# First expert's counts in narrow products, row of -1 in the operand, tokens turned on PE, constant fill in attention, and both stages in a new order

## The chip, the cores and the metric

One Trainium2 chip, one of its cores. The engines of the core are PE (TensorE; its weight loads are shown apart as PEld), DVE (VectorE), ACT (ScalarE), POOL (GpSimd) and SP (SyncE), which issues most DMAs. The metric is the time of one execution on the device in microseconds (us); the kernel's time is the median of several runs.

## What is computed

Top-32 attention over 8 batches and 8 heads (576 positions, 64 dimensions a head), then a mixture of 8 experts over the 4608 tokens, to which tokens go by a greedy assignment in order of their logits, at most 576 to an expert.

```python
def _attn_ref(q, k, v):
    scores = scale * np.matmul(q, k.transpose(0, 1, 3, 2))
    kth = np.partition(scores, -top_k, axis=-1)[..., -top_k:-top_k + 1]
    scores = np.where(scores >= kth, scores, -1000000000.0)
    ...
    return np.matmul(attn, v)

def _moe_ref(x, w_gate, w1, w2):
    logits = x @ w_gate
    order = np.argsort(-logits.flatten())
    for idx in order:
        tok, e = (int(idx) // E, int(idx) % E)
        if assigned[tok] >= 0 or counts[e] >= cap:
            continue
        assigned[tok] = e
        counts[e] += 1
    for e in range(E):
        mask = assigned == e
        out[mask] = np.maximum(x[mask] @ w1[e], 0.0) @ w2[e]
```

## The kernel before

**Order.** Both stages are written as operations with a due time: `at(t, f, pre, e=...)` registers operation `f` for engine `e`. `Plan.run` simulates the engines and issues, on each one, among the operations that could begin within `WIN` of the earliest, the one of smallest due time. The due time is the tile's or expert's own time plus an offset from the table `O`. The result is a fixed stream of instructions for each engine, which then runs in that order. `PLANBUFS` and the arguments of the second `Plan` give the sizes of the rings of buffers. So a new table gives a new order without any other change.

**Attention** runs over 32 pairs (8 batches, 4 pairs of heads) with 9 tiles of 128 rows each, 288 in all. Q and K are loaded, rounded on POOL and turned by DMA transposes on SP (line 186). For a tile PE writes 128x576 scores in `s` (218). DVE finds the largest values in six chunks (221), ranks them (224 to 228), and writes the negative of the 24th value (229). ACT takes the sign of every score against it and sums that in `acc` (233). PE moves the scores above it far down with a product by `off` (236), and DVE's `fill` (238) puts up to eight copies of the 24th value in the eight columns behind the scores, as many as the sum in `acc` asks for. DVE's next MAX8 (239) takes eight values over 584 columns; PE moves the others back with `back` (236), and ACT clears what is below the 32nd (242). Then come the masked scores once more, transposed (PE, 285 and 286), the exponential (ACT, 290), its two halves in f16 (POOL, 293 and 296), the products with V (PE, 364), the reciprocal of the sum (DVE, 344 and 378) and the scaled rows in `x` (ACT, 346).

After the fourth pair of a batch, `logits` (388) turns the batch's rows on PE in five pieces (396), copies them to SBUF on ACT (398), multiplies them by the gate's weights on PE (402, 404) and puts 8 columns in `L` on ACT (407, 408). The pieces wait for the pair's last rows. `verdict` (416) follows the planned part in program order: it checks `acc` with eight operations (420 to 428) and `L` for values that are not finite (430 to 432), and writes flags. `redo` reads the flags and branches to a repeat, or goes on.

**Experts.** Expert p has a `route`: six steps that close in on its threshold. In a step DVE compares all best logits with 32 thresholds (`g`, 671; three parts for the first expert), PE counts with 9 products that hold four tiles each (674), DVE masks and folds (677, 680), PE sums them up (684) and writes -1 in the columns next to them (685, with a constant row `mone`), DVE compares with the capacity (687, `okb`), PE adds that on the -1 (688), and DVE takes the largest (689) and the next thresholds (695, 696). `enlist` (738) makes the list of the expert's tokens: DVE writes one-hot tiles (757 to 761), PE lays them out (`lay`, 36 products, 765) and spreads them (772), DVE forms `idx` (775). `weigh` (776) reads the expert's number on SP (779), loads four weight blocks of 1 MB (787, ring of four buffers `wr`) and splits them into two f16 halves (ACT 799, DVE 807). `bring` (822) gathers the tokens on POOL in five tiles (829), splits them (ACT 836, DVE 839, ring of three `xs`), and turns them with DMA transposes on SP (840). `ffn` (841) multiplies: 192 products `ph` (856), their halves (ACT 865, DVE 866), 108 steps of `po` (880, 883), the result (890 to 894) and a scatter on POOL (895). The next expert's route, list and weights are planned beside the products of the one before.

## Time and profile before

| | us |
|---|---|
| median of 3 runs | 1474.12 |
| the runs | 1474.12, 1472.0, 1474.5 |
| the profiled execution, its own time | 1470.44 |
| its span | 1468.4 |
| PE busy | 1295.9 (88%) |
| PE weight loads (PEld) busy | 913.2 (62%) |
| DVE busy | 1220.3 (83%) |
| POOL busy | 877.2 (60%) |
| ACT busy | 864.6 (59%) |

The profile is of one execution. The busy shares are means over the stages: attention takes the time up to about 964, the route and fetch of the first expert up to about 1028, and the experts' products the rest.

### The profile page before, as it was taken

Reading aid. Unit: us, or ns where it says so; the run is one execution under the profiler, and the core shown is the slowest. Engines: PE = TensorE matmul, PEld = TensorE weight load, DVE = VectorE, ACT = ScalarE, POOL = GpSimd, SP = SyncE. Lnnn points to the kernel's source line nnn. Section 1 sums busy time; section 2 is a strip of 40 time slices with the busy share of each in tenths; the row PEclk is TensorE's granted clock in tenths of the full one; section 3 lists DMA queues with packets and bytes.
Section 4 is the critical chain, followed back from the end, with each engine's and each line's share of the span. In section 5 each row is a group of like instructions: output and inputs, shape, how many; then the busy total and the mean of one; then the engine's idle time right before and its main releaser. Section 6 shows DMA issues by size and latency. Waiting matters only on the chain. (4 is left out here: it accounts for less than half of the span.)

```text
span 1468.4 us, 41338 instructions
## 1 busy us (share of the span) xinstructions
PE 1295.9 (88%) x14885; PEld 913.2 (62%) x14886; DVE 1220.3 (83%) x5951; ACT 864.6 (59%) x1922; POOL 877.2 (60%) x1285
## 2 busy tenths in 40 slices
PE   2888998999999999999999899832999999998997
PEld 1666776776776776677677677621655655664663
DVE  4899999999999999999999999658889878887610
ACT  2677777777777777777777787612334424324421
POOL 5688789788788788789879878502043123122211
PEclk9899999999999999999999999955999999999899
DMA  6343363354455445443543452016346346348500
GB/s 130 74 88 78 80 127 84 75 120 91 82 110 97 89 108 84 94 109 77 97 110 83 92 107 46 10 35 170 122 99 198 137 91 198 140 96 271 112 33 33
DMA packets 298149, 149.62 MB, mean 102 GB/s; under 512 B 255440, under 2 KB 280016, under 8 KB 296912
## 3 DMA queue, kind: packets, MB, share of 16 engines
q1 hardware_dynamic: 292048, 128.02, 38.5%
q0 software_dynamic: 5888, 18.88, 4.5%
q8 instruction: 119, 1.95, 0.6%
q14 instruction: 94, 0.77, 0.2%
HBM read 71.34 MB, written 18.87 MB: 61 GB/s over the span
## 5 line engine op out<-in xcount | busy, mean ns | idle before, releaser
L221 DVE MAX8 cd<-s 128x8 f32<-128x96 f32 x1728 | 383.2, 251 | 35.4 <-PE s L218 28.6
L296 POOL TENSOR_TENSOR elm<-F,ehm 128x512 f16<-128x512 f32 x256 | 294.3, 1156 | 6.3
L242 ACT ACTIVATE r<-s,st 128x576 bf16<-128x576 f32 x288 | 213.0, 740 | 98.8 <-PE s L236 93.8
L233 ACT ACTIVATE w<-s,st 128x576 uint16<-128x576 f32 x288 | 213.1, 740 | 95.0 <-DVE st L229 92.9
L895 POOL DMA_INDIRECT out_dram<-ob,idx x40 | 59.0, 1476 | 326.1 <-ACT ob L890 268.2
L239 DVE MAX8 st<-s 128x8 f32<-128x584 f32 x288 | 220.5, 766 | 10.4 <-PE s L236 6.7
L218 PE MATMUL s<-K,Q 128*128 128x512 f16 (+3 forms) x1280 | 195.3, 293 | 28.6 <-DMA Q<-nq 22.3
L856 PE MATMUL ph<-xT,w1h 128*128 128x288 f16 x1024 | 195.8, 289 | 2.0 <-DMA xT<-xs 2.0
L293 POOL TENSOR_SCALAR ehm<-F 128x512 f16<-128x512 f32 x256 | 156.0, 617 | 52.7 <-ACT F L290 52.3
L286 PE MATMUL pt<-Q,K 66*128 66x128 f16 (+1 forms) x1280 | 182.6, 217 | 0.2 <-DMA Q<-nq 0.2
L285 PE MATMUL pt<-Q,K 128*128 128x128 f16 (+1 forms) x1280 | 181.6, 216 | 0.0
L218 PEld LDWEIGHTS <-Q 128*128 128x128 f16 (+1 forms) x1280 | 105.9, 103 | 111.9 <-DMA Q<-nq 22.0
L236 PE MATMUL s<-w,off 128*128 128x512 f16 x576 | 134.1, 290 | 46.8 <-DVE s L238 26.9
L290 ACT ACTIVATE F<-pt 128x512 f32<-128x512 f32 x256 | 150.4, 596 | 20.8 <-PE pt L286 18.5
L856 PE MATMUL ph<-xT,w1l 128*128 128x288 f16 x512 | 147.6, 288 | 0.0
L364 PE MATMUL pv<-vt,E 128*64 128x65 f32 (+1 forms) x1024 | 146.4, 257 | 0.0
L236 PE MATMUL s<-w,back 128*128 128x512 f16 x576 | 120.9, 292 | 23.5 <-DVE st L239 21.7
L865 ACT ACTIVATE hh<-ph 128x288 f16<-128x288 f32 x128 | 52.4, 410 | 146.3 <-PE ph L856 145.4
L285 PEld LDWEIGHTS <-K 128*128 128x128 f16 x1280 | 118.3, 99 | 22.5 <-issue 8.7
L364 PEld LDWEIGHTS <-ehm 128*128 128x128 f16 x2048 | 116.2, 102 | 10.0 <-issue 0.5
L364 PEld LDWEIGHTS pv<-vt,E 128*64 128x64 f32 (+1 forms) x1024 | 113.0, 164 | 14.5 <-issue 3.5
L364 PE MATMUL pv<-vh,ehm 128*128 128x65 f16 x1024 | 120.8, 195 | 0.6 <-ACT F L290 0.6
(252 smaller groups left out, 3271.0 us busy)
## 6 DMA issues: line engine op xcount, KB each, us to landing
wr<-in_moe_w_dram SPq DMA_DIRECT2D x32, 1024.0 KB, 8.2
kn<-in_k_dram SPq DMA_DIRECT2D x64, 128.0 KB, 2.6
qn<-in_q_dram SPq DMA_DIRECT2D x64, 128.0 KB, 2.3
vn<-in_v_dram SPq DMA_DIRECT2D x64, 128.0 KB, 2.3
x<-xb SPq DMA_DIRECT2D x8, 1024.0 KB, 4.8
Q<-nq SPq DMA_TRANSPOSE x160, 3.3
kn<-in_k_dram SPq DMA_DIRECT2D x64, 16.0 KB, 2.3
qn<-in_q_dram SPq DMA_DIRECT2D x64, 16.0 KB, 2.2
```

The costliest lines, as they stand in the source:

```text
L218: T.matmul(s_ps[rows,a:b_],P[Q][:,qc],P[K][:,h*576+a:h*576+b_],start=(Q=="Q1"),stop=(Q=="Q2"))
L221: V.max(D["cd"][:,c*8:c*8+8],D["s"][:,576*c//NCH:576*(c+1)//NCH])
L233: A.activation(D["w"],D["s"][:,:576],AF.Sign,bias=P["st"][:,i,32:33],scale=(1+2.0**-21),accum_out=acc[:,col])
L236: T.matmul(D["s"][:,a:b_],by,w[:,a:b_],start=False,stop=True,skip_group_check=True)
L239: def next8(): V.max(P["st"][:,i,24:32],D["s"][:,:584])
L242: A.activation(r,D["s"][:,:576],AF.Relu,bias=P["st"][:,i,31:32],scale=-1.0)
L285: T.matmul(o,K2[:,kb:kb+128],Q1[:,qc],start=False,stop=False,skip_group_check=True)
L286: T.matmul(o,K3[0:66,kb:kb+128],Q2[0:66,qc],start=False,stop=(c==3 and h==sub[-1][0]),skip_group_check=True)
L293: G.tensor_scalar(D["eh"],D["E"],1.0,0.0,op0=ALU.mult,op1=ALU.add)
L296: G.tensor_tensor(el,D["E"],D["eh"],op=ALU.subtract); P["e"][i]=(D["eh"],el)
L364: for m_ in (range(N-1) if part==0 else (N-1,)): T.matmul(out,seq[m_][0],seq[m_][1],start=(m_==0),stop=(m_==N-1))
L856: P.matmul(B["ph"][:,:288],a[:,c,fs],xT[:,b+c,cs],start=(i==0),stop=(i==11))
```

## The change

In attention, `fill` writes a constant, 2^40, in place of the row's 24th value, so it reads one scalar of each partition fewer; the relu and the planner's durations are otherwise as before. `logits` is in two parts: after a batch's third pair it turns and multiplies the first 384 of 512 columns of each row group (four pieces) and one corner, and copies the results to `L`; after the fourth pair it does the last 128 columns of all four row groups in one piece and the second corner, and adds them to `L`. These copies and adds are on DVE, no longer on ACT. `verdict` tests `L` in four pieces (12 operations) and folds its flags in other operations. In the experts, `okb` has a 33rd row that holds -1 in two fixed buffers, so the product with `mone` is gone and the product with `okb` stands alone. The first expert's counts are 36 products of 128x32 weights that add up in one tile of 32x8, without the mask, the two folds and the sum. The first expert's tokens are turned by PE in place of DMA: four transposes a tile into PSUM, from which ACT and DVE write the two halves. The tables `O`, `PER`, `SP` and `WIN` of attention and the tables of the experts have other numbers, and with them all engines have another order.

```diff
-        PER=4.6166; SP=1.3822; VP=3; WPB=14; EHB=14
-        WIN={'V': 0.027, 'A': 0.079, 'G': 0.008, 'P': 0.138, 'D': 1.472}
+        PER=4.9146; SP=1.9733; VP=3; WPB=14; EHB=14
+        WIN={'V': 0.021, 'A': 0.06, 'G': 0.042, 'P': 0.137, 'D': 1.95}
...
-            def fill(): V.tensor_scalar(D["s"][:,576:584],tab,acc[:,col],P["st"][:,i,23:24],op0=ALU.is_lt,op1=ALU.mult)
+
+            def fill(): V.tensor_scalar(D["s"][:,576:584],tab,acc[:,col],2.0**40,op0=ALU.is_lt,op1=ALU.mult)
...
-        def logits(P):
-            b=P["b"]; n=P["n"]; t0=(n*9+8)*PER+O["lg"]
-            fin=[]
-            for c in range(5):
-                p=P["done"]
-                D={}; w=512 if c<4 else 256
-                def turn(c=c,D=D):
-                    D["pt"]=ps_t.tile([128,512],F32,tag="pt",name="ptl")
-                    for f in range(4 if c<4 else 2): T.transpose(D["pt"][:,f*128:(f+1)*128],P["x"][0][:,c,f*128:(f+1)*128] if c<4 else P["x"][1][:,2*f:2*f+2,:].rearrange("p a d -> p (a d)"),identf)
-                def copy(D=D,w=w):
+        def logits(P,part):
+
+            b=P["b"]; n=P["n"]; t0=(n*9+8)*PER+O["lg"]; o=(b%2)*64
+            done=P["done"]; fin=[]
+            def piece(k,turns,w,dots,put):
+
+                D={}; t=t0+O["lgd"]*k
+                def turn():
+                    pt=D["pt"]=ps_t.tile([128,512],F32,tag="pt",name="ptl")
+                    for j,src in enumerate(turns): T.transpose(pt[:,j*128:j*128+128],src(),identf)
+                def copy():
                     D["xT"]=wk.tile([128,512],F32,tag="xT",name="xT",bufs=2); A.activation(D["xT"][:,:w],D["pt"][:,:w],AF.Copy)
-                def dot(c=c,D=D):
-                    lg=D["lg"]=ps_t.tile([128,512],F32,tag="pt",name="lg"); xT=D["xT"]; o=(b%2)*64
-                    if c<4:
-                        for f in range(4): T.matmul(lg[:,:8],xT[:,f*128:(f+1)*128],wg[:,f,:],start=(f==0),stop=(f==3))
-                    else:
-                        for i_,(g,a) in enumerate(((0,0),(0,1),(1,0),(1,1))): T.matmul(lg[o:o+64,:8],xT[:,g*128+a*64:g*128+a*64+64],wgr[:,g,a,:],start=(i_==0),stop=(i_==3))
-                def put(c=c,D=D):
-                    o=(b%2)*64
-                    if c<4: A.activation(L[:,b*4+c,:],D["lg"][:,:8],AF.Copy)
-                    else: A.activation(L[o:o+64,32+b//2,:],D["lg"][o:o+64,:8],AF.Copy)
-                t=t0+O["lgd"]*c
-                p=at(t,turn,[p],take="pt",e="P",d=.436); tp=p
-                p=at(t+O["l1"],copy,[p],free=[tp],take="xT",e="A",d=.48); tx=p
-                p=at(t+O["l2"],dot,[p],take="pt",free=[tx],e="P",d=.9); tp=p
-                p=at(t+O["l3"],put,[p],free=[tp],e="A",d=.07); fin.append(p)
-            P["fin"]=at(t0,lambda: None,fin)
-            P["done"]=p
+                def dot():
+                    D["lg"]=ps_t.tile([128,512],F32,tag="pt",name="lg"); dots(D["lg"],D["xT"])
+                p=tp=at(t,turn,[done],take="pt",e="P",d=.11*len(turns))
+                p=tx=at(t+O["l1"],copy,[p],free=[tp],take="xT",e="A",d=.06+w*.00083)
+                p=tp=at(t+O["l2"],dot,[p],take="pt",free=[tx],e="P",d=.224*len(turns))
+                fin.append(at(t+O["l3"],lambda: put(D["lg"]),[p],free=[tp],e="V",d=.08))
+            main=L[:,b*4:b*4+4,:]; last=L[o:o+64,32+b//2,:]
+            def corner(g):
+                def dots(lg,xT):
+                    for a in range(2): T.matmul(lg[o:o+64,:8],xT[:,a*64:a*64+64],wgr[:,g,a,:],start=(a==0),stop=(a==1))
+                return [lambda: P["x"][1][:,2*g:2*g+2,:].rearrange("p a d -> p (a d)")],128,dots
+            if part==0:
+                for c in range(4):
+                    def dots(lg,xT):
+                        for f in range(3): T.matmul(lg[:,:8],xT[:,f*128:f*128+128],wg[:,f,:],start=(f==0),stop=(f==2))
+                    piece(c,[lambda f=f,c=c: P["x"][0][:,c,f*128:f*128+128] for f in range(3)],384,dots,lambda lg,c=c: V.tensor_copy(L[:,b*4+c,:],lg[:,:8]))
+                piece(4,*corner(0),lambda lg: V.tensor_copy(last,lg[o:o+64,:8]))
+            else:
+                def dots(lg,xT):
+                    for c in range(4): T.matmul(lg[:,c*8:c*8+8],xT[:,c*128:c*128+128],wg[:,3,:],start=True,stop=True)
+                piece(0,[lambda c=c: P["x"][0][:,c,384:512] for c in range(4)],512,dots,lambda lg: V.tensor_tensor(main.rearrange("p c e -> p (c e)"),lg[:,:32],main.rearrange("p c e -> p (c e)"),op=ALU.add))
+                piece(1,*corner(1),lambda lg: V.tensor_tensor(last,lg[o:o+64,:8],last,op=ALU.add))
+            P["fin"]=at(t0,lambda: None,fin); P["lgdone"]=fin[-1]
...
-            Lf=L.rearrange("p t e -> p (t e)"); fin=cp.tile([128,Lf.shape[1]],F32,name="fin")
-            V.tensor_tensor(fin,Lf,Lf,op=ALU.subtract)
-            V.tensor_scalar(fin,fin,0.0,None,op0=ALU.is_equal)
-            V.tensor_reduce(good[:,npr:],fin,axis=AX.X,op=ALU.add)
+            whole=[]
+            for k,(u0,u1) in enumerate(((0,28),(32,35),(28,32),(35,36))):
+                Lf=L[:,u0:u1,:].rearrange("p t e -> p (t e)"); w=8*(u1-u0); fin=cp.tile([128,w],F32,name=f"fin{k}")
+                V.tensor_tensor(fin,Lf,Lf,op=ALU.subtract)
+                V.tensor_scalar(fin,fin,0.0,None,op0=ALU.is_equal)
+                V.tensor_reduce(good[:,npr+k:npr+k+1],fin,axis=AX.X,op=ALU.add); whole.append(128.0*w)
...
-            if P["hp"]==3 or n==len(pairs)-1:
-                logits(P); batch[b]=at((n*9+8)*PER+O["lg"]+O["lgd"]*5,lambda P=P: store(P),[P["fin"]],e="D",d=2.0,late=4.0)
+            if P["hp"]==2: logits(P,0)
+            if P["hp"]==3:
+                P["done"]=at(P["done"]["t"]+.001,lambda: None,[P["done"],Ps[n-1]["fin"]])
+                logits(P,1); P["done"]=P["fin"]; batch[b]=at((n*9+8)*PER+O["lg"]+O["lgd"]*5,lambda P=P: store(P),[P["fin"]],e="D",d=2.0,late=4.0)
...
+        okbs=[cp.tile([T+1,E],BF16,name=f"okb{k}") for k in range(2)]
+        for t in okbs: V.memset(t[T:T+1,:],-1.0)
...
-                    def begin(): o("g",128,NT,T,dt=BF16); D_["pc"]=new(ps,[128,512],F32,"pc",1)
+                    def begin(p=p):
+                        o("g",128,NT,T,dt=BF16); D_["pc"]=new(ps,[128,512],F32,"pc",1)
+                        if p==0: D_["pn"]=D_["pc"]
                     for q in range(pcs):
                         js=slice(q*n,q*n+n)
                         def cmp_(q=q,js=js):
@@ -671,21 +688,25 @@
                             V.tensor_tensor(D_["g"][:,js,:],D_["v"][:,js].unsqueeze(2).to_broadcast([128,n,T]),D_["thr"].unsqueeze(1).to_broadcast([128,n,T]),op=ALU.is_ge)
                         cq=plan.at(c.t+.05*q,cmp_,head+(R["span"] if p==0 and s==0 else []),e="V",d=.07+n*T*.00104,order=[cq] if q else []); cv=[cq]
                         def count(q=q):
-                            for j in range(q*n,q*n+n,4): P.matmul(D_["pc"][:,:32],D_["g"][:,j:j+4,:].rearrange("p a b -> p (a b)"),D_["ohb"][:,j:j+4,:].rearrange("p a b -> p (a b)"),start=(j==0),stop=(j==NT-4))
-                        mms.append(plan.at(c.t,count,cv+(mms[-1:]),e="P",d=.03*(n//4)+.03))
+                            if p==0:
+                                for j in range(q*n,q*n+n): P.matmul(D_["pn"][:T,:E],D_["g"][:,j,:],D_["ohb"][:,j,:],start=(j==0),stop=(j==NT-1))
+                            else:
+                                for j in range(q*n,q*n+n,4): P.matmul(D_["pc"][:,:32],D_["g"][:,j:j+4,:].rearrange("p a b -> p (a b)"),D_["ohb"][:,j:j+4,:].rearrange("p a b -> p (a b)"),start=(j==0),stop=(j==NT-4))
+                        mms.append(plan.at(c.t,count,cv+(mms[-1:]),e="P",d=.03*(n//4)+.03 if p else .03*n+.03))
                     c.pre=[mms[-1]]; c.t+=.15
-                    c.add("V",.10,lambda: V.tensor_tensor(o("cm",128,32),D_["pc"][:,:32],dm,op=ALU.mult))
-                    def fold():
-                        o("ch",128,E,dt=F16)
-                        with nc.allow_low_precision(reason="counts up to 1152"): V.tensor_reduce(D_["ch"],D_["cm"].rearrange("p (j e) -> p e j",e=E),axis=AX.X,op=ALU.add)
-                    c.add("V",.10,fold)
-                    def total():
-                        D_["pn"]=new(ps,[128,512],F32,"pc",1)
-                        P.matmul(D_["pn"][:T,:E],sel_,D_["ch"],start=True,stop=True)
-                        P.matmul(D_["pn"][:,16:16+E],onesb[:1,:],mone,start=True,stop=False,skip_group_check=True)
-                    c.add("P",.06,total)
-                    c.add("V",.07,lambda: V.tensor_scalar(o("okb",T,E,dt=BF16),D_["pn"][:T,:E],float(CAP),None,op0=ALU.is_ge))
-                    c.add("P",.04,lambda: P.matmul(D_["pn"][:,16:16+E],onesb[:T,:],D_["okb"],start=False,stop=True,skip_group_check=True))
+                    if p:
+                        c.add("V",.10,lambda: V.tensor_tensor(o("cm",128,32),D_["pc"][:,:32],dm,op=ALU.mult))
+                        def fold():
+                            o("ch",128,E,dt=F16)
+                            with nc.allow_low_precision(reason="counts up to 1152"): V.tensor_reduce(D_["ch"],D_["cm"].rearrange("p (j e) -> p e j",e=E),axis=AX.X,op=ALU.add)
+                        c.add("V",.10,fold)
+                        def total():
+                            D_["pn"]=new(ps,[128,512],F32,"pc",1)
+                            P.matmul(D_["pn"][:T,:E],sel_,D_["ch"],start=True,stop=True)
+                        c.add("P",.06,total)
+                    def enough(s=s): D_["okb"]=okbs[(s+p)%2]; V.tensor_scalar(D_["okb"][:T,:],D_["pn"][:T,:E],float(CAP),None,op0=ALU.is_ge)
+                    c.add("V",.07,enough)
+                    c.add("P",.04,lambda: P.matmul(D_["pn"][:,16:16+E],onesb[:T+1,:],D_["okb"],start=True,stop=True,skip_group_check=True))
...
+                if p==0:
+                    B={}
+                    def turn(j=j,n=n,B=B):
+                        if j==0: e["xT"]=new(sm,[128,8,CAP],F16,"xT")
+                        B["pt"]=new(ps,[128,512],F32,"ph",4).rearrange("p (f n) -> p f n",f=4)
+                        for f in range(4): P.transpose(B["pt"][:,f,:n],xgs[j][:n,f*128:f*128+128],ident[:n,:n])
+                    def hi(j=j,n=n,B=B): A.activation(e["xT"][:,0:4,j*128:j*128+n],B["pt"][:,:,:n],AF.Copy,scale=SX)
+                    def lo(j=j,n=n,B=B): V.scalar_tensor_tensor(e["xT"][:,4:8,j*128:j*128+n],B["pt"][:,:,:n],SX,e["xT"][:,0:4,j*128:j*128+n],op0=ALU.mult,op1=ALU.subtract)
+                    tp=plan.at(t+.1*j+.01,turn,[g],e="P",d=.45,take="ph",free=[g],order=[e["x"][j-1] if j else None])
+                    if j==0: te=plan.at(t+.1*j+.015,lambda: None,[tp],take="xT"); e["txT"]=te
+                    a=plan.at(t+.1*j+.02,hi,[tp,te],e="A",d=.5)
+                    e["x"].append(plan.at(t+.1*j+.03,lo,[a],e="V",d=.6,free=[tp]))
+                    continue
```

The table `O` of the experts (line 595) changes in the same way as the one of attention, and the durations given for fill and next8 are 0.12 and 0.685 in place of 0.075 and 0.735. Below is what the new tables give at three places.

DVE, at the end of attention, before: `rs` belongs to the scaling of the last values, `vc`, `vr`, `vok` and `good` to the check of `acc`, `fin` to that of `L`.

```order
L344 TENSOR_SCALAR rs_21723<-pv_21705 128x1
L378 RECIPROCAL rs_21723<-rs_21723 128x1
L420 TENSOR_SCALAR vc_21793<-acc_158 128x288
L421 TENSOR_SCALAR vr_21794<-vc_21793 128x288
L422 TENSOR_SCALAR vr_21794<-vr_21794 128x288
L423 TENSOR_TENSOR vok_21795<-vr_21794,vc_21793 128x288
L424 SCALAR_TENSOR_TENSOR vok_21795<-vc_21793,vok_21795 128x288
```

The same place after:

```order
L345 TENSOR_SCALAR rs_21844<-pv_21828 128x1
L379 RECIPROCAL rs_21844<-rs_21844 128x1
L417 COPY L_61<-lg_21841 64x8
L421 TENSOR_TENSOR L_61<-lg_21860,L_61 128x32
L422 TENSOR_TENSOR L_61<-lg_21865,L_61 64x8
L428 TENSOR_SCALAR vc_21873<-acc_158 128x288
L429 TENSOR_SCALAR vr_21874<-vc_21873 128x288
L430 TENSOR_SCALAR vr_21874<-vr_21874 128x288
```

The last copy of `L` and the two adds now stand between the last values and the check of `acc`.

SP, at the fetch of the seventh expert, before: `wr` are weight blocks of the eighth expert, `xT` and `xs` the seventh expert's tokens, five tiles in order.

```order
L787 DMA wr_27883<-in_moe_w1_dram 128x2x1024
L840 DMA_TRANSPOSE xT_27896<-xs_27897 128x8x128
L787 ISA
L787 DMA wr_27938<-in_moe_w2_dram 128x4x512
L840 DMA_TRANSPOSE xT_27896<-xs_27933 128x8x128
L840 DMA_TRANSPOSE xT_27896<-xs_27953 128x8x128
L840 DMA_TRANSPOSE xT_27896<-xs_27973 128x8x128
L840 DMA_TRANSPOSE xT_27896<-xs_27993 128x8x64
```

The same place after:

```order
L808 DMA wr_28035<-in_moe_w1_dram 128x2x1024
L874 DMA_TRANSPOSE xT_28003<-xs_28004 128x8x128
L874 DMA_TRANSPOSE xT_28003<-xs_28038 128x8x128
L808 ISA
L808 DMA wr_28093<-in_moe_w2_dram 128x4x512
L874 DMA_TRANSPOSE xT_28003<-xs_28062 128x8x128
L874 DMA_TRANSPOSE xT_28003<-xs_28100 128x8x128
L874 DMA_TRANSPOSE xT_28003<-xs_28126 128x8x64
```

The second tile's transpose has moved ahead of the third weight block.

PE, at the first expert's first products, after (before, the products `ph` there stand alone behind a step of counts): line 860 are the turns, `pc` the second expert's counts.

```order
L694 MATMUL pc_23556<-ohb_23477,g_23555 128x32
L860 MATMUL ph_23583<-identm_63,xg_23539 128x128 x4
L860 MATMUL ph_23595<-identm_63,xg_23547 128x128 x4
L705 LDWEIGHTS sel_118
L705 MATMUL pc_23604<-ch_23600,sel_118 32x8
L860 MATMUL ph_23607<-identm_63,xg_23552 128x128 x4
L890 LDWEIGHTS w1h_23443
L890 MATMUL ph_23617<-xT_23559,w1h_23443 128x288
```

The turns of the second to fourth tile stand ahead of the first product; the fifth comes a few products later. At the start of the program SP now issues the second Q transpose (line 186) directly behind the first; before, four loads of the next pair's k (158, 159) stood between them.

## Rows read from the trace of the kernel before

**Rows 1.** The page: busy time of the engines, and the granted clock in slices.
```profile
PE 1295.9 (88%) x14885; PEld 913.2 (62%) x14886; DVE 1220.3 (83%) x5951; ACT 864.6 (59%) x1922; POOL 877.2 (60%) x1285
...
PEclk9899999999999999999999999955999999999899
```

**Rows 2.** Windows: stretch, length, busy time by engine, clock, DMA share, GB/s.
```profile
200.00:400.00 200.00, 185.97 (x2518) 140.72 (x2516) 187.65 (x1053) 153.58 (x361) 168.49 (x261) 0.99 0.44 92
980.00:1000.00 20.00, 6.61 (x63) 3.75 (x63) 15.23 (x60) 0.00 (x0) 0.00 (x0) 0.50 0.00 0
1358.00:1364.00 6.00, 4.29 (x31) 2.67 (x32) 4.26 (x9) 0.00 (x0) 1.48 (x1) 0.50 0.79 232
```

**Rows 3.** Timeline of the prologue on SP and PE: start, length, engine, line, operation, [idle before].
```profile
16.64 0.59 SPq L158 DMA_DIRECT2D kn<-in_k_dram  x1
...
19.00 1.33 SPq L186 DMA_TRANSPOSE Q<-nq  x1
...
22.29 3.06 PE L218 MATMUL s<-K,Q 128*128 128x512 f16 x12 [22.29 <-DMA Q<-nq]
```

**Rows 4.** Timeline of DVE: a fill, and a 128x8 operation with one scalar.
```profile
930.24 0.29 DVE L238 TENSOR_SCALAR s<-tab,acc,st 128x8 f32<-128x8 f32 x1 [0.16 <-ACT w L233]
...
1002.45 0.22 DVE L735 TENSOR_SCALAR w8c<-rev,win 128x8 f32<-128x8 f32 x1
```

**Rows 5.** Timeline of the end of attention on DVE and PE.
```profile
954.31 0.29 DVE L420 TENSOR_SCALAR vc<-acc 128x288 f32<-128x288 f32 x1
...
957.36 0.45 DVE L428 TENSOR_REDUCE good<-vok 128x32 f32<-128x288 f32 x1
...
964.14 0.46 DVE L430 TENSOR_TENSOR fin<-L 128x288 f32<-128x288 f32 x1 [6.33 <-ACT L L408]
...
967.13 0.14 DVE L443 CAST flags<-bad 1x1 int32<-1x1 f32 x1
...
954.35 1.16 PE L396 MATMUL ptl<-identf,xb 128*128 128x128 f32 x8 [0.35 <-ACT xb L346]
...
955.69 1.95 PE L402 MATMUL lg<-wg,xT 128*128 128x8 f32 x16 [0.18 <-ACT xT L398]
```

**Rows 6.** Waits from 100 to 900: us in total, times, longest us.
```profile
PE s L236 <- DVE s L238: 21.1, 72, 0.7
...
PEld lg L402 <- ACT L L407: 3.3, 5, 0.7
```

**Rows 7.** Timeline of the first expert's route and list, on DVE and PE.
```profile
981.25 1.50 DVE L671 TENSOR_TENSOR g<-v,thr 128x384 bf16<-128x384 f32 x3
...
983.90 0.15 DVE L687 TENSOR_SCALAR okb<-pc 32x8 bf16<-32x8 f32 x1 [0.37 <-PE pc L685]
...
1007.54 0.76 PE L765 MATMUL pl<-bt,ah 128*32 128x40 bf16 x18 [6.34 <-DVE bt L761]
```

**Rows 8.** Timeline of the first expert's fetch on ACT and its first product.
```profile
1024.81 0.63 ACT L836 ACTIVATE xs<-xg 128x512 f16<-128x512 f32 x1 [2.16 <-DMA xg<-x,idx]
...
1027.87 0.64 PE L856 MATMUL ph<-xT,w1h 128*128 128x288 f16 x2 [2.00 <-DMA xT<-xs]
```

**Rows 9.** Timeline of the expert stage; the last row is of the chain.
```profile
1100.63 0.17 PE L685 MATMUL pc<-mone,onesb 1*128 1x8 bf16 x1
1100.73 0.42 PE L856 MATMUL ph<-xT,w1h 128*128 128x288 f16 x2
...
1346.49 12.23 SPq L840 DMA_TRANSPOSE xT<-xs  x4
...
1356.81 0.68 DVE L839 SCALAR_TENSOR_TENSOR xs<-xg,xs 64x512 f16<-64x512 f32 x1 [4.21 <-ACT xs L836]
...
1359.71 0.76 PE L765 MATMUL pl<-bt,ah 128*32 128x40 bf16 x18 [8.09 <-DVE bt L761]
...
1435.14 10.36 PE po L880 x48
```

25 lines of the change are left out of this document (13 added, 12 removed).

## The prediction

> **What bounds the kernel now.** I read the page first. PE is busy 1295.9 us of 1468.4, and the granted clock's slices fall to half at one place only, where attention hands over to the experts [rows 1]. A share of busy time hides stages, so I read the windows next. In the middle of attention 200 us hold 185.97 of PE and 187.65 of DVE: the two engines are at 93% and 94% together, and the order that the planner wrote keeps each waiting a little for the other [rows 2]. Around 980 to 1000, in the route of the first expert, DVE is busy 15.23 of 20 and everything else stands: a serial chain of compare, count and decide, at half clock [rows 2]. In the expert stage PE is the engine that is nearly always busy; where it stops, the cause is a list or a transfer. So I split the time into prologue, attention, its end, the first expert's route and fetch, and the expert stage, and cost the edits in each. The sum is made against the profiled execution, 1470.44 us; the median of the runs shown is 1474.12, 3.7 more, and the runs spread over 2.5. About 0.2%, 3 us, is what a measurement of this kernel can tell from no change.
>
> **Prologue: -2.** PE's first scores wait until 22.29 for a Q transpose. SP issues the first one at about 16.6, then four loads of the next pair's k, and the second at 19.00 [rows 3]. The new order puts the two transposes back to back, so the second can go 2.4 earlier, and it takes as long to land as before. Ends 0 (its input is the limit) and -2.4; I take -2.
>
> **Attention: -9.** Fill reads two scalars of each partition and takes 0.29; the nearest operation with the same 128x8 tile and one such scalar takes 0.22 [rows 4]. Over 288 tiles that saves 17.3 (0.06 each) to 20.2 (0.07). Against it, the results of the logits no longer go to L through ACT, 40 times, but through DVE, 7 per batch, 56 times. No row of before has that operation; the small cast of 1x1 took 0.14 [rows 5] and the 128x8 fill without its second scalar 0.22 [rows 4], so 7.8 to 12.3, and I take 0.14, since copies and adds read no scalar. Net on DVE -9.5, ends -12.4 and -5. Does it reach the end? PE waits 72 times, 21.1 in all over 800 us, for just this fill [rows 6], and DVE is the busier of the two, so yes unless the new order gives PE longer waits; 7% of PE's time is idle, some 65 us over the stage, which is room for 9. Zero is the end on that side. The split of the logits in two moves about three quarters of their PE work (12 of 16 transposes and one corner of two) ahead by a pair; products and transposes are the same in number to within a few, so PE's sum stays. ACT, 59% busy, loses 40 small puts that hide anyway: nothing.
>
> **End of attention and flags: 0.** Before, the last batch's logits run from 954.35 behind the last values, and L is whole when DVE starts at 964.14. The eight operations on acc, 954.31 to 957.36 and 0.45 more, cost nothing, since they fill DVE's wait of 6.33 [rows 5]. After, only the second part follows the last values: four transposes (half of 1.16, 0.58), a copy 0.6, four products (a quarter of 1.95, 0.5), their neighbours in the corner, an add, some 4.5 with the hand-overs. L would be whole at 958.9, 5.2 sooner. But the DVE order puts the operations on acc behind the adds, so that 3.5 loses its cover, and the finite test of L grows from three operations of up to 0.46, about 1.3, to twelve smaller ones, at some 0.24 each (an estimate between 0.14 and 0.46) 2.9: 3.5 + 1.6 = +5.1. The two cancel; ends -2 and +2.
>
> **Route of the first expert: -3.** One step goes from the end of the compare (981.25 + 1.50 = 982.75) over nine products, two folds on DVE and a total to okb at 983.90: 1.15 [rows 7]. After, the last third's 12 small products stand there alone. Eighteen products with 32 weight columns took 0.76 in the list, 0.042 each [rows 7], so 0.5 and 0.1 to hand over: 0.6, which saves 0.55 in each of six steps. The other end is the spacing of a lone product between products, 0.10 (1100.63 to 1100.73) [rows 9], by which 12 cost 1.2 and the step grows by 0.15, +0.9 in all. The list's row has the same 32 weight columns and comes in one unbroken run, as these do, so I take -3.
> The Trainium skill, "TensorE: Matmul & The Clock Gate", section "LDWEIGHTS (loading the stationary operand)", has the load grow with the columns alone (27 ns for 32, an estimate by its formula), and section "Weight-path perf modes — Fast Weight Load (FWL) and DoubleRow" gives the fast load only to 128 weights, which speaks against 36 narrow ones. By its formula, an estimate, 12 loads would be 0.32 and the step would save 0.7 in place of 0.55; the listed 0.042 is longer, and the measurement decides.
>
> **Fetch of the first expert: -3.** PE starts the first expert at 1027.87, after 2.00 of waiting for the DMA transposes; the fourth tile's rows had landed by 1024.81 [rows 8]. After, PE turns each tile (half of 1.16, 0.58), ACT reads it 0.63, DVE 0.68. PE's order has the fourth tile's turn ahead of the first product, so the start is 1024.8 plus a fraction, 1024.4 to 1025.4. Ends -1 (ACT and DVE late) and -5 (the turn of the fourth is early).
>
> **The -1 product: -3.6.** 36 of 42 products of mone lie in the expert stage, where PE is the bound, and each moves the next product by 0.10 (1100.63 to 1100.73) [rows 9]. Removed: -3.6. The row of -1 is written once, and 33 rows instead of 32 cost nothing more.
>
> **Stall before the seventh expert: -6.** PE stands 8.09 at 1359.71 for the list of the eighth expert, at half clock after it (4.29 busy in 6 us, about 2 of it lost) [rows 2, 9]. Backwards: the list's DVE work stands behind the seventh expert's last xs at 1356.81, which waited 4.21 for ACT, which waited for a transpose; the SP queue held four transposes from 1346.49 for 12.23, behind a weight load [rows 9]. In the new SP order two transposes stand ahead of that load instead of one, so the last xs needs no transpose that is queued behind it: -4.2 to -4.6. PE has 75 po products between the lists in place of 63; at 10.36 for 48, 0.216 each [rows 9], 2.6 more cover. Together 7 of the 8.09. But the third to fifth transposes are still behind the load, and the seventh's products need them: that is late next, so I take -6, ends 0 and -10 (with the clock).
>
> **Sum.** -2 -9 +0 -3 -3 -3.6 -6 = -26.6. 1470.4 - 26.6 = 1443.8, and 3.7 for the median: **1447.5**.
>
> **The rivals.** (1) *The stall stays.* SP's transposes and loads share one queue, and four transposes took 12.23 behind one load [rows 9]. If two transposes behind two loads land as late as one did, xs waits again and the 6 stays: 1453.5. For: the two loads ahead are the same. Against: the second transpose is now ahead of the third load.
> The Trainium skill, "DMA: Bandwidth & Descriptors", section "Queues, rings and completion order", says that SP owns one row of rings and that each engine consumes descriptors in ring order; by that rule the transposes behind a load wait for all of it, and the time is this rival's 1453.5 unless the order puts them ahead. The 12.23 agrees.
> (2) *DVE's saving is not passed on*: the new attention order gives PE other waits, term 0 in place of -9: 1456.5; with (1) 1462.5. For: PE is at 93%. (3) *The new order gains more*: besides the fill's own time half of the 21.1 that PE waits for it goes as well: 1447.5 - 10.5 = 1437. (4) *The copies of L block DVE*, slower: DVE issues in order, and the copy stands ahead of the selection's operations. If its dot is late, DVE waits, as PE's load of lg did for ACT's put, up to 0.7 in 5 cases [rows 6]. At 0.7 of waiting and 0.14 of work, 56 cost 47 and attention goes from -9 to about +29.7: 1447.5 + 38.7 = 1486. It decides from 0.14 + 26.6 / 56 = 0.62 each. Against: five of the seven now stand beside the following pair's work, where the dots have time. (5) *Nothing comes of it*: attention 0, the stall unchanged and the first expert's gains lost to a list that comes no earlier: within 3 of 1474.
>
> **How the numbers follow.** Forecast 0.40, (1) 0.20, (2) with or without (1) 0.15, (3) 0.12, (5) 0.05, (4) 0.08. Faster by over 0.2%: the first four, 0.87; within 0.05; slower 0.08. The range takes the first four: down from 1437 to 1430, for the ends of the fetch (-2), the fill (-3) and the clock (-2), and up from 1462.5 to 1466, for the route (+3.9 at its worst). Left out are (4), (5) and the far ends, under 2 in 10.
>
> **What the next profile would show.** Fill near 0.22 and the DVE copies near 0.14, with no wait of 0.6 before them; DVE's share in 200 to 400 down by about a point, and PE's waits for fill below 21.1. The second Q transpose near 16.6 and first scores near 20. Steps of the first route 0.5 shorter, with 12 small products in about 0.5; if they take over 1.1, that term was wrong. First expert's first product some 3 us sooner after its list. No product of mone. PE's longest wait for a list below 2.5, and a clock of one there. The prediction falls if attention's length moves by over 5 from -9, since no other term is as large, or if a new wait of several us stands ahead of another expert.

## The result, and the profile after

The changed kernel takes 1456.31 us in the median (four runs, 1453.31 to 1458.44) where the kernel before takes 1474.31 (1472.0 to 1478.34): a ratio of 0.9874, with an interval of 0.9845 to 0.9902. The forecast was 1447.5 with a range of 1430 to 1466. The direction and the range held; of the 26.6 us expected, 18.0 came in the medians. The profiled execution took 1456.97, a span of 1455.2, so the two profiled executions are 13.5 apart and their spans 13.2: the profiled run of the kernel before, 1470.44, is shorter than each of its four timed runs. Attention's length differs by up to 5 us from one execution to the next: the kernel before's last reciprocal is at 954.23, and in two other profiles below that leave its attention untouched, it came at 954.54 and 958.98.

The place where each stage ends, in both traces, tells where the time went. The last column is what the sum had for it. A list counts as there when DVE forms `idx` from it.

| stage | before | after | moved | forecast |
|---|---|---|---|---|
| start to first scores | 22.29 | 20.25 | -2.0 | -2 |
| to the last reciprocal of attention | 931.94 | 922.63 | -9.3 | -9 |
| to the flags | 13.04 | 11.74 | -1.3 | 0 |
| to the experts' first operation on DVE | 4.76 | 5.50 | +0.7 | 0 |
| to the first expert's list | 40.30 | 36.60 | -3.7 | -3 |
| to its first product | 15.54 | 12.94 | -2.6 | -3 |
| to the last product | 430.43 | 435.75 | +5.3 | -9.6 |
| to the end of the span | 10.1 | 9.8 | -0.3 | 0 |

Up to the first expert's first product the change had gained 18.2, and 17 were forecast. All that is missing between these two profiles, 13.4, was lost behind it, in the expert stage, which is 14.9 longer than forecast.

The page of after, against [rows 1] (busy time of each engine, the granted clock in slices):

```profile
PE 1291.6 (89%) x15019; PEld 908.3 (62%) x15020; DVE 1208.0 (83%) x6010; ACT 863.5 (59%) x1898; POOL 878.1 (60%) x1285
...
PEclk8899999999999999999999999955999999999999
```

Timeline of after at the start and at the end of attention, against [rows 3, 5] (start, length, engine, line, operation, idle before and what ended it):

```profile
15.50 2.74 SPq L186 DMA_TRANSPOSE Q<-nq  x2
...
20.25 3.06 PE L218 MATMUL s<-K,Q 128*128 128x512 f16 x12 [20.25 <-DMA Q<-nq]
...
942.88 0.16 DVE L379 RECIPROCAL rs<-rs 128x1 f32<-128x1 f32 x1
...
946.05 0.19 DVE L421 TENSOR_TENSOR L<-lg,L 128x32 f32<-128x32 f32 x1 [2.81 <-PE lg L420]
...
946.76 0.31 DVE L428 TENSOR_SCALAR vc<-acc 128x288 f32<-128x288 f32 x1
...
954.46 0.16 DVE L454 CAST flags<-flf 1x32 int32<-1x32 f32 x1
```

Both Q transposes now go together. L is whole at 946.75, 3.9 behind the last reciprocal in place of 9.9, and the check of acc begins only then.

DVE's groups in after, against [rows 4] (count, busy us, mean ns, idle before), and its wait with PE against [rows 6] (total, times, longest):

```profile
L239 DVE TENSOR_SCALAR s<-tab,acc 128x8 f32<-128x8 f32 x288 | 63.8, 222 | 10.9 <-ACT w L233 6.4 <-PE s L236 0.9
...
L416 DVE COPY L<-lg 128x8 f32<-128x8 f32 x32 | 4.9, 153 | 1.6 <-PE lg L415 1.6
...
L421 DVE TENSOR_TENSOR L<-lg,L 128x32 f32<-128x32 f32 x8 | 1.5, 182 | 2.8 <-PE lg L420 2.8
```

```profile
PE s L236 <- DVE s L239: 22.2, 51, 1.0
```

Fill takes 222 ns in place of 281 in the mean, 17 us less over 288. PE waits for it as long as before in total (22.2 and 21.1), in fewer and longer waits.

Route and first product of the first expert in after, against [rows 7, 8]:

```profile
968.68 1.50 DVE L688 TENSOR_TENSOR g<-v,thr 128x384 bf16<-128x384 f32 x3
...
969.29 1.42 PE L692 MATMUL pc<-ohb,g 128*32 128x8 bf16 x36 [1.14 <-DVE g L688]
...
970.75 0.15 DVE L707 TENSOR_SCALAR okb<-pc 32x8 bf16<-32x8 f32 x1 [0.17 <-PE pc L692]
...
971.64 1.50 DVE L688 TENSOR_TENSOR g<-v,thr 128x384 bf16<-128x384 f32 x3
...
1008.75 1.12 PE L860 MATMUL ph<-identm,xg 128*128 128x128 f32 x4 [0.18 <-DMA xg<-x,idx]
1009.66 0.69 PE L890 MATMUL ph<-xT,w1h 128*128 128x288 f16 x2
```

A step is 2.96 long (968.68 to 971.64) where it was 3.55; 36 narrow products take 1.42, 0.039 each.

PE's longer waits in the expert stage of after, where before had one of 8.09 [rows 9] and none of the others over 1.4:

```profile
1067.35 0.40 PE L890 MATMUL ph<-xT,w1h 128*128 128x288 f16 x2 [2.24 <-DMA xT<-xs]
...
1069.17 0.26 PE L694 MATMUL pc<-ohb,g 128*128 128x32 bf16 x3 [1.29 <-DVE g L688]
...
1118.02 0.17 PE L705 MATMUL pc<-ch,sel 128*32 128x8 f16 x1 [1.00 <-DVE ch L701]
...
1177.06 0.24 PE L694 MATMUL pc<-ohb,g 128*128 128x32 bf16 x3 [3.48 <-DVE g L688]
...
1340.58 0.38 PE L914 MATMUL po<-w2h,hh 128*128 128x512 f16 x1 [1.38 <-DVE ob L928]
...
1344.63 0.74 PE L786 MATMUL pl<-bt,ah 128*32 128x40 bf16 x18 [1.95 <-DVE bt L782]
```

Windows of after around two of them (length, busy time of PE, PEld, DVE, ACT and POOL, granted clock, DMA share, GB/s):

```profile
1065.00:1081.00 16.00, 12.26 (x90) 8.25 (x89) 10.79 (x31) 3.17 (x7) 2.68 (x2) 0.79 0.31 76
1173.00:1185.00 12.00, 8.52 (x45) 3.50 (x44) 8.71 (x22) 1.45 (x3) 1.95 (x2) 0.86 0.37 99
```

The 8.09 became 1.38 and 1.95. But PE now waits near the second expert's start (1067 to 1069) and ahead of the fourth's (1177) as well, and after these waits the granted clock is at its lower level for 6.8 us (from 1068.2) and 3.4 us (from 1177.5), so they cost more than their own length. What DVE and ACT did ahead of these waits, and two later places:

```profile
1067.96 0.68 DVE L873 SCALAR_TENSOR_TENSOR xs<-xg,xs 64x512 f16<-64x512 f32 x1 [2.51 <-ACT xs L870]
...
1174.42 0.63 ACT L870 ACTIVATE xs<-xg 64x512 f16<-64x512 f32 x1 [4.11 <-DMA xT<-xs]
1175.08 0.68 DVE L873 SCALAR_TENSOR_TENSOR xs<-xg,xs 64x512 f16<-64x512 f32 x1 [3.37 <-ACT xs L870]
1175.69 0.24 DVE L717 SCALAR_TENSOR_TENSOR thr<-stp,mx,base 128x32 f32<-128x32 f32 x1
...
1176.46 1.48 DVE L688 TENSOR_TENSOR g<-v,thr 128x384 bf16<-128x384 f32 x3
...
1229.94 0.68 DVE L873 SCALAR_TENSOR_TENSOR xs<-xg,xs 64x512 f16<-64x512 f32 x1 [1.00 <-ACT xs L870]
...
1282.64 0.68 DVE L873 SCALAR_TENSOR_TENSOR xs<-xg,xs 64x512 f16<-64x512 f32 x1 [1.30 <-ACT xs L870]
```

At 1175 DVE stands idle 3.37 for the split of the fourth expert's fifth tile (its 64 rows). The next thresholds and the compare of the following expert's route stand behind it in program order, and PE's count behind the compare. At the second expert DVE stands 2.51 in the same way, ahead of the compare, and at the fifth and sixth 1.00 and 1.30 ahead of other operations of a step: 8.2 in all.

### The profile page after: what moved, and what is told of

The parts are those of the page before. It is cut to its first block, busy times and chain, and to the rows that moved or that the text cites. A ratio compares the mean times of both kernels' runs of the same rounds, so it can differ in the third digit from the quotient of the medians.

```text
span 1455.2 us, 41655 instructions
## 1 busy us (share of the span) xinstructions
PE 1291.6 (89%) x15019; PEld 908.3 (62%) x15020; DVE 1208.0 (83%) x6010; ACT 863.5 (59%) x1898; POOL 878.1 (60%) x1285
## 5 line engine op out<-in xcount | busy, mean ns | idle before, releaser
L221 DVE MAX8 cd<-s 128x8 f32<-128x96 f32 x1728 | 373.5, 252 | 35.3 <-PE s L218 30.6
L929 POOL DMA_INDIRECT out_dram<-ob,idx x40 | 54.9, 1372 | 223.8 <-ACT ob L924 157.4
L287 PE MATMUL pt<-Q,K 66*128 66x128 f16 (+1 forms) x1280 | 179.1, 216 | 0.1
L286 PE MATMUL pt<-Q,K 128*128 128x128 f16 (+1 forms) x1280 | 178.2, 215 | 0.0
L850 POOL DMA_INDIRECT xg<-x,idx x40 | 51.7, 1292 | 179.0 <-DVE idx L796 107.3
L365 PEld LDWEIGHTS pv<-vt,E 128*64 128x64 f32 (+1 forms) x1024 | 113.2, 164 | 13.5 <-issue 3.1
```

Of the source, the lines that this page charges most:

```text
L221: V.max(D["cd"][:,c*8:c*8+8],D["s"][:,576*c//NCH:576*(c+1)//NCH])
L286: T.matmul(o,K2[:,kb:kb+128],Q1[:,qc],start=False,stop=False,skip_group_check=True)
L287: T.matmul(o,K3[0:66,kb:kb+128],Q2[0:66,qc],start=False,stop=(c==3 and h==sub[-1][0]),skip_group_check=True)
L365: for m_ in (range(N-1) if part==0 else (N-1,)): T.matmul(out,seq[m_][0],seq[m_][1],start=(m_==0),stop=(m_==N-1))
```

## The experiments

Times of experiments are compared with runs of the kernel before on the same chip (1472 to 1474 in the median). First product to last product is called the stage; it is 430.4 before and 435.8 after.

**Which half of the change lost it.** The new attention with the old experts:

```diff
-        PER=4.6166; SP=1.3822; VP=3; WPB=14; EHB=14
+        PER=4.9146; SP=1.9733; VP=3; WPB=14; EHB=14
...
-            def fill(): V.tensor_scalar(D["s"][:,576:584],tab,acc[:,col],P["st"][:,i,23:24],op0=ALU.is_lt,op1=ALU.mult)
+            def fill(): V.tensor_scalar(D["s"][:,576:584],tab,acc[:,col],2.0**40,op0=ALU.is_lt,op1=ALU.mult)
...
-        def logits(P):
+        def logits(P,part):
...
```

The lines are against the kernel before; all of the change in `attention` is in, and `moe` stays as it was.

> The attention of the changed kernel with the experts of the kernel before. Theory: attention, its end and the prologue gave all that the change gained (flags written 12.6 us sooner), and the experts' edits and new order net nearly nothing (5 sooner up to the first product, 5 lost after it): the time is that of the changed kernel within 3 us, a span near 1456, with first product to last product at 430 as before. Rival: the 5 us that the expert stage lost come from what stands ahead of it and not from its own order: then the stage is 435 here too and the span near 1461.

It took 1456.04 us, span 1454.5, stage 430.9. The theory holds: against the kernel before's 1472.18 the new attention and what it leaves gave 16.1 (0.9884, 0.9861 to 0.9907), which is the change's 18.0 (0.9874) within the intervals, and the whole new expert part gave about nothing. The 435.8 of the change's stage are the experts' own.

**The row of -1 alone**, in the kernel before:

```diff
-                        P.matmul(D_["pn"][:,16:16+E],onesb[:1,:],mone,start=True,stop=False,skip_group_check=True)
...
-                    c.add("P",.04,lambda: P.matmul(D_["pn"][:,16:16+E],onesb[:T,:],D_["okb"],start=False,stop=True,skip_group_check=True))
+                    c.add("P",.04,lambda: P.matmul(D_["pn"][:,16:16+E],onesb[:T+1,:],D_["okb"],start=True,stop=True,skip_group_check=True))
```

> The kernel before with the row of -1 in the operand and without the product of mone, nothing else. Theory: each of 36 products in the expert stage held PE for 0.10, so first product to last product falls from 430.4 by 3.4 to 427.0. Rival: the product fitted into time that PE had, and the wait before the eighth expert's list grows by what is saved: the stage stays within 1 of 430.4.

The stage is 427.0, as the theory had it; the median 1466.92 against 1472.18 (ratio 0.9972, 0.9956 to 0.9988).

**The constant in fill alone**, in the kernel before, with its order:

```diff
-            def fill(): V.tensor_scalar(D["s"][:,576:584],tab,acc[:,col],P["st"][:,i,23:24],op0=ALU.is_lt,op1=ALU.mult)
+            def fill(): V.tensor_scalar(D["s"][:,576:584],tab,acc[:,col],2.0**40,op0=ALU.is_lt,op1=ALU.mult)
```

> The kernel before with the constant in fill alone; every engine's order as it was. Theory: DVE sets attention's pace, so most of 288 x 0.06 = 17 us of DVE time comes through: the last reciprocal (954.2 before) comes 8 to 17 sooner. Rival: in the old order PE and the waits between the two take it up: under 4 sooner.

It took 1459.25 against 1472.25 (0.9911, 0.9876 to 0.9947), 13 us from one operand, as the theory had it. The last reciprocal:

```profile
941.89 0.16 DVE L378 RECIPROCAL rs<-rs 128x1 f32<-128x1 f32 x1
```

It comes 12.3 sooner than before (954.23), of 17 that DVE saves. In the changed kernel it came 11.4 sooner, the 2 of the prologue included. From the first scores to the last reciprocal it is 919.6 here, and 921.0 in the run with all edits in the old orders below, which has the same attention; it is 921.5 to 923.5 in six traces with the change's attention (this change, and the runs below that leave its attention and its end as they are, with the new attention and the old experts among them). So the split of the logits and attention's new table together took back some 2.

**Attention's old table** under the edits of the change:

```diff
-        PER=4.9146; SP=1.9733; VP=3; WPB=14; EHB=14
-        WIN={'V': 0.021, 'A': 0.06, 'G': 0.042, 'P': 0.137, 'D': 1.95}
+        PER=4.6166; SP=1.3822; VP=3; WPB=14; EHB=14
+        WIN={'V': 0.027, 'A': 0.079, 'G': 0.008, 'P': 0.138, 'D': 1.472}
...
```

> The changed kernel with attention's tables (PER, SP, WIN, O) of the kernel before; the edits stay. Theory: the gain in attention is the edits' (fill less, copies of L more): the last reciprocal is at about 945 to 947, 2 of the 11.4 lost with the second Q transpose. Rival: the order brought it, and with the old table the copies of L on DVE wait for their products: 954 or later.

The last reciprocal is at 961.37 and the median 1475.95, above the kernel before (1.0022, 1.0001 to 1.0043). The rival holds. The groups of L on DVE in this kernel:

```profile
L416 DVE COPY L<-lg 128x8 f32<-128x8 f32 x32 | 4.8, 151 | 4.4 <-PE lg L415 4.2
...
L421 DVE TENSOR_TENSOR L<-lg,L 128x32 f32<-128x32 f32 x8 | 1.5, 189 | 4.8 <-PE lg L420 4.8
...
L417 DVE COPY L<-lg 64x8 f32<-64x8 f32 x8 | 1.3, 163 | 4.6 <-PE lg L410 4.6
```

The copies are about as short as in the changed kernel, but DVE stands 13.8 in all ahead of them (some 4.5 there, 2.8 of it after the last values). This is the prediction's fourth rival in kind, seen under the old order: the split of the logits needs the new table, and with it costs and brings about as much. The last reciprocal is 19.5 later than with the constant alone; the waits of DVE are the larger part of that, and the rest was not taken apart.

**The turn on PE undone** in the changed kernel (DMA transposes for the first expert):

```diff
-                if p==0:
-                    B={}
...
-                    continue
```

> The changed kernel with DMA transposes for the first expert's tokens as before. Theory: the turn's gain is given back at the second expert, whose list hangs on the route and not on the first expert's products: first product 2 to 3 later than 1009.7, second expert's first product within 1 of 1067.4 with PE's wait of 2.2 gone, span within 2. Rival: the gain is real to the end: the span grows by 3.

It took 1457.07, span 1454.8: with this table the change is no slower without the turn, as the theory says. Where the gain is lost is not where the theory put it. The first product comes 4.0 later and the second expert's 4.3 later (1071.68), so the gain is still there; the third expert's comes 0.6 later and the fourth's 2.9 sooner (1126.70 and 1181.64, against 1126.11 and 1184.53 with the turn). The stage is 431.4. The planner writes another order when the turn is gone (at least 153 of DVE's 1078 operations in the experts change place), so this compares the turn and its order with the transposes and theirs, not the turn alone.

**The experts' old table** under the edits of the change: only the numbers of O in `moe` are those of before.

```diff
-        O=dict(RT=341.23, TE=-289.219, TN=-172.671, WT=261.813, XT=32.643, RD=-297.654, GL=2.6, W_V=0.1, W_A=0.395, W_G=2.142, W_P=0.0, W_D=9.225, WD0=678.788, WD1=322.634, RA=-247.153, WT0=9.992, TE0=-55.559, XT0=-502.675)
+        O=dict(RT=274.437, TE=-46.447, TN=-90.531, WT=82.391, XT=-180.56, RD=-288.435, GL=2.6, W_V=0.099, W_A=2.033, W_G=0.144, W_P=0.0, W_D=0.747, WD0=757.588, WD1=237.776, RA=-374.027, WT0=-194.686, TE0=-40.731, XT0=-156.385)
```

> The changed kernel with the experts' tables of the kernel before; the edits stay. Theory: the new table brought the waits before the second, third and fourth experts' work and took the one before the seventh: with the old one, the 8.1 before the eighth expert's list is back, the 2.2 and 3.5 are gone, and first product to last product is 427 to 431, below the 435.8 of the changed kernel. Rival: the edits brought those waits, and the stage is 435 or more with the 8.1 on top.

It took 1446.22 (ratio 0.9811, 0.9785 to 0.9838), 10 below the change. The theory holds. The stage is 427.5, PE's waits of 3.48 and 1.29 are gone and the 2.24 is 0.76, DVE stands 0.4 in all for the fifth tiles of the second to sixth experts, and the old wait is back:

```profile
1337.19 0.76 PE L786 MATMUL pl<-bt,ah 128*32 128x40 bf16 x18 [8.61 <-DVE bt L782]
```

So the experts' edits are worth about what was forecast: the stage is 3 shorter than before, which is the row of -1, and from the first list to the first product it is 11.4 where before had 15.5, the part that the turn changes. The new order of the experts cost 10, though it took 5 off one stall.

**All edits but the split of the logits, both old tables:**

```diff
-            def fill(): V.tensor_scalar(D["s"][:,576:584],tab,acc[:,col],P["st"][:,i,23:24],op0=ALU.is_lt,op1=ALU.mult)
+            def fill(): V.tensor_scalar(D["s"][:,576:584],tab,acc[:,col],2.0**40,op0=ALU.is_lt,op1=ALU.mult)
...
+        okbs=[cp.tile([T+1,E],BF16,name=f"okb{k}") for k in range(2)]
...
+                            if p==0:
+                                for j in range(q*n,q*n+n): P.matmul(D_["pn"][:T,:E],D_["g"][:,j,:],D_["ohb"][:,j,:],start=(j==0),stop=(j==NT-1))
...
```

The lines are against the kernel before; all of the change in `moe` but its table O is in.

> The kernel before with all edits of the change but the split of the logits and its check (logits as before on ACT), and with both stages' old tables. Theory: the constant in fill (-13), the row of -1 (-3.4), the narrow counts (-3.5) and the turn (-2 to -4) add up and need no new table: 1472.3 - 22 to -24 = 1448 to 1450, faster than the change by 6 to 8. The split of the logits with attention's new table is then worth 2 to 4, the distance to 1446.2. Rival: without the new tables the edits' gains are given back as new waits, and the time is 1456 or more.

It took 1448.16 (0.9814, 0.978 to 0.9848): the theory holds. Four small edits in the old order beat the change by 8, though the two intervals just meet.

**Five xs buffers**, in the changed kernel and in the kernel before, no other order:

```diff
-                    xss[j]=new(sm,[128,2,D],F16,"xs",3)
+                    xss[j]=new(sm,[128,2,D],F16,"xs",5)
```

> The changed kernel with a ring of five xs buffers in place of three, every engine's order as it was. Theory: DVE's waits for the last tile's split (3.4 before the count step at 1177, 3.9 before the list at 1340) come from the ring, which makes ACT wait for a DMA transpose, and PE's waits of 3.5, 1.4 and 2.0 come from those: they go, with the half clock behind them, and the span falls by 6 to 9 to about 1448. Rival: the transposes are next late, PE waits at the first product of those experts for the DMA instead, and the span falls by under 2.

> The kernel before with a ring of five xs buffers, the order as it was. Theory: the wait of 4.2 of DVE for the seventh expert's last split goes, and with it 4 to 8 of PE's 8.1 before the eighth expert's list and 2 of half clock: the span falls by 6 to 10. Rival: the queue of transposes behind the weight block is the cause and the seventh expert's first product waits for it all the same: under 2.

The theory falls in both. In the changed kernel the span is 1451.9, 3.3 shorter where the theory had 6 to 9 and the rival under 2, and the median 1453.15 (0.9865, 0.9842 to 0.9888), 3 below the change and within its interval. PE still waits 3.06 for the count near 1175:

```profile
1172.30 0.63 ACT L870 ACTIVATE xs<-xg 64x512 f16<-64x512 f32 x1 [4.26 <-DMA xg<-x,idx]
1172.96 0.68 DVE L873 SCALAR_TENSOR_TENSOR xs<-xg,xs 64x512 f16<-64x512 f32 x1 [3.33 <-ACT xs L870]
1173.57 0.24 DVE L717 SCALAR_TENSOR_TENSOR thr<-stp,mx,base 128x32 f32<-128x32 f32 x1
```

In the change ACT waited here for a transpose, to have a buffer of the ring (4.11 above). With the ring out of the way the fifth split waits for its gather, nearly as long (3.33 on DVE in place of 3.37), and PE has waits of 2.09 and 2.62 at other steps that the change did not have. In the kernel before the list's wait falls from 8.09 to 3.12, and 1.70 come back where the products wait for the transposes:

```profile
1363.42 0.61 PE L765 MATMUL pl<-bt,ah 128*32 128x40 bf16 x18 [3.12 <-DVE bt L761]
1366.59 0.64 PE L856 MATMUL ph<-xT,w1h 128*128 128x288 f16 x2 [1.70 <-DMA xT<-xs]
```

The stage is 428.5 there, 2 shorter; the median 1469.56 (0.9976, 0.9959 to 0.9993). The ring is a cause of some of the waits (the stage of the changed kernel falls from 435.8 to 431.4 with five), but not of the whole loss.

**The fifth split behind the next step**, in the changed kernel. The planner took 2.6 us for a gather to land; it is told 6.5 for the fifth tile of the second to eighth experts, and so writes the split later: behind the compare of the following expert's step at the second and fourth experts, and behind other operations of a step at the third, fifth and sixth, each time in exchange with splits of weights. At least 36 of DVE's 1078 operations in the experts, 6 of ACT's and 42 of PE's 3481 products change place with that, none of POOL's or SP's:

```diff
-                g=plan.at(t+.1*j,lambda j=j: gather(j),[e["idx"]],e="G",d=1.04,take="xg",late=GL,order=[g,prev])
+                g=plan.at(t+.1*j,lambda j=j: gather(j),[e["idx"]],e="G",d=1.04,take="xg",late=GL if j<4 or p==0 else 6.5,order=[g,prev])
```

> The changed kernel, with the planner told that the gather of an expert's fifth tile lands 6.5 us after its issue and not 2.6 (the trace shows some 6). In DVE's order the fifth split then stands behind the next thresholds and the compare of the following expert's route at three experts, among them the place at 1177; nearly all else keeps its order. Theory: DVE stood there for the fifth tile, first for the ring and, with five buffers, for the gather, and the route's step stood behind it: the 3.5 that PE waits at 1177 falls below 0.7, with 1.5 to 2 of half clock behind it, and the span by 3 to 5, to about 1451. Rival: the step is late for its own reasons, or the split that is now later holds the second half of the products: PE waits as long at the same place or some 10 us later, and the span falls by under 1.

It took 1442.98 (0.9799, 0.977 to 0.9828), span 1440.1, stage 421.6. The theory holds, and its size was far too small: the span fell by 15 where it had 3 to 5. The same place:

```profile
1165.33 0.24 DVE L717 SCALAR_TENSOR_TENSOR thr<-stp,mx,base 128x32 f32<-128x32 f32 x1
...
1166.10 1.48 DVE L688 TENSOR_TENSOR g<-v,thr 128x384 bf16<-128x384 f32 x3
...
1167.63 0.68 DVE L873 SCALAR_TENSOR_TENSOR xs<-xg,xs 64x512 f16<-64x512 f32 x1
```

```profile
1166.70 0.24 PE L694 MATMUL pc<-ohb,g 128*128 128x32 bf16 x3 [0.49 <-DVE g L688]
```

And the windows that answer to the two of after:

```profile
1065.00:1081.00 16.00, 15.63 (x145) 11.64 (x145) 13.65 (x44) 4.21 (x10) 0.98 (x1) 1.00 0.20 55
1163.00:1175.00 12.00, 11.51 (x78) 5.78 (x77) 10.96 (x29) 2.65 (x5) 4.17 (x3) 1.00 0.68 115
```

Compare, thresholds and split come without a wait, DVE stands nowhere for a fifth tile of the second to sixth experts, the clock stays at its upper level, and PE's waits of 1.29, 1.00, 3.48 and the smaller ones behind them are gone or under 0.5. The wait for the second expert's transposes, 2.24, stays at 1.89, and the two ahead of the eighth expert's list are 1.52 and 1.95. From the first product of one expert to that of the next it is 56.6, 53.4, 53.8, 53.1 and 53.4 for the first five experts, where the change has 57.7, 58.8, 58.4, 54.9 and 54.3: a step that comes late makes the next expert's list late as well. The third expert's list is there 99.1 behind the first product in the change and 93.7 with the late split.

The two traces account for the whole difference. In the stage PE's idle time is 14.2 in the change and 6.1 with the late split, and the clock is at its lower level for 17.6 and 5.0. By an estimate that counts half of the time at the lower level as lost, that is 23.0 against 8.6, a difference of 14.4; the stages differ by 14.1. So what the planner took for the fifth tile's landing cost 14 of the stage. That it was the place of this split, and not of the other operations that moved with it, is argued from DVE's waits, 8.2 against none, and was not tested by moving the split alone.

**The check of acc ahead of the last adds.** With the experts' old table, the check of acc, the finite test of the parts of L that are whole by then, and the constants are planned as DVE work behind the last tile of attention:

```diff
+        def ahead(last):
...
+            for f in fs: p=at(1e6,f,[p] if p else last,e="V",d=.4)
...
+        ahead([P["rel"][i] for i in range(9)]+[P["clear"],Ps[len(pairs)-5]["fin"]])
         loom.run()
         verdict()
```

> The changed kernel with the experts' old tables, and with the check of acc and two thirds of the finite test of L (fourteen of the twenty operations, and the constants) planned as DVE work of its own while the last values run, instead of behind the last adds of L. Theory: these 5 us have no cover behind the adds and find one in DVE's waits for the last values, so the flags come 4.5 to 5.5 sooner after the last reciprocal (11.6 before the edit) and the median is 1441, 5 below the kernel with old tables alone (1446.2). Rival: they delay the last reciprocals or PE's next work, or the branch behind the flags waits for something else, and under 2 come through.

> The same with a ring of five xs buffers and the same order. Theory: as in the kernel before, the ring takes 5 of the 8.6 that PE waits for the eighth expert's list, and 1.7 come back as a wait for the transposes, 2 to 3 in all with a little of the clock: median 1438 to 1439. Rival: the list waits for the weight blocks too and the gain is under 1.

The first took 1443.85 (0.9794, 0.9771 to 0.9817). The flags come 7.6 behind the last reciprocal, which was 11.6 under the old experts' table without this edit, so 4.0 came, a little under the theory; the median is 2.4 below that kernel's 1446.22, where 5 were expected, and the intervals overlap:

```profile
942.22 0.16 DVE L379 RECIPROCAL rs<-rs 128x1 f32<-128x1 f32 x1
...
946.19 0.19 DVE L421 TENSOR_TENSOR L<-lg,L 128x32 f32<-128x32 f32 x1 [3.61 <-PE lg L420]
946.91 0.19 DVE L429 TENSOR_TENSOR fin<-L 128x32 f32<-128x32 f32 x1
...
949.62 0.16 DVE L456 CAST flags<-flf 1x32 int32<-1x32 f32 x1
```

With five buffers on top it took 1437.66 (five runs, 1436.6 to 1442.83; ratio 0.9757, 0.9735 to 0.978), the fastest median here, 19 below the change. Its profile shows the wait for the eighth list at 2.79 and 1.52 of waiting for the transposes behind it, where the kernel with three has 7.65, but also 2.69 more at another expert's step, and its profiled execution is no shorter (span 1441.0 against 1439.4). How much of the 6 between the medians is the ring's is open, and whether the theory of 2 to 3 holds is not shown. No run joins the late split to the early check.

## Why the prediction was right, and where it was not

The steps up to the experts' products were right, most to within a microsecond. **Prologue** -2.0. **Attention** -9.3 for -9, but by other parts than the sum had, so that the two agree is in part luck: fill saved the 17 on DVE, the copies and adds of L take 153 and 182 ns, 8.8 in all, near the lower end of the bounds, and DVE's time does set the pace; yet the constant alone brought 12.3 in the old order, not 17, and the rest, logits and new table, took back some 2, where the sum had charged 7.8 for the copies. The length before is itself 931.9 to 936.8 from trace to trace. PE's waits for fill, which were to fall below 21.1, are 22.2. **End of attention** -1.3 for 0: L came 6.0 sooner behind the last reciprocal, and the check of acc, without its cover, gave most of it back, as worked out. The last experiment shows that its place was the cause. **Route** 0.59 a step for 0.55; the 12 products of the last part take 0.47 by the measured 0.039. The estimate from the Trainium skill, "TensorE: Matmul & The Clock Gate", section "LDWEIGHTS (loading the stationary operand)", 27 ns a load, would have been 0.32. The trace at the lower clock has 39 ns a product, so the measurement decides against it. **Fetch** -2.6 for -3. **The -1 product** -3.4 alone for -3.6.

**The stall before the seventh expert** went from 8.09 to 3.3, in two pieces, 4.8 of the -6 that was taken; the clock around it is at its lower level for 3.4 us in place of 10.2, where the prediction had a clock of one. It did not go quite by the step's own way. The step had the last split need no transpose that is queued behind a load; but ACT still waits for a transpose ahead of the fourth tile, and DVE with it:

```profile
1339.12 0.69 DVE L873 SCALAR_TENSOR_TENSOR xs<-xg,xs 128x512 f16<-128x512 f32 x1 [3.85 <-ACT xs L870]
```

Before, DVE stood 1.77 for the fourth tile and 4.21 for the fifth. How the 4.8 divide between this and the longer cover on PE was not tested.

What failed is what stood beside this step: the sum followed the new order of the experts only at the one wait that the trace of before showed, and carried every other expert at no change. It checked what the new order would remove and not what it would put in. The prediction named a new wait of several us ahead of another expert as what would make it wrong; it gave that no term, no rival and no price. The runs price it: the new table cost 10 against the old one, and with the late split the stage is 421.6, against 420.8 by the sum (430.4 - 3.6 - 6). So the edits' terms had about the right size, and the missing term, +14, is the order around the fifth splits, for which DVE stood 8.2 at the second, fourth, fifth and sixth experts.

Of the rivals, (1) came in part: a split waits for a transpose again, 3.85 in place of 4.21, but PE's stall fell by more than half all the same. (2) did not come as worded: the 9 were passed on, though the fill's saving was passed on less fully than the sum had it. (4) came under the old table only. That no rival was about the new experts' table is the gap in the list.

That the time lies in the range is in part luck: the missing 14 were less than the 15 that the range left above the forecast for rivals (1) and (2) together, and the reasons did not foresee them.
